# A retention layer in front of two MLPs: the first chunks' scores weighted by a decay table instead of scaled q and v

## The chip, the cores and the metric

The kernel runs on one core of one Trainium2 chip. The time is the device time of one execution in microseconds (us); the span of a profile is the part of it from the first to the last instruction. The engines are TensorE (PE; its weight loads PEld), VectorE (DVE), ScalarE (ACT), GpSimd (POOL) and SyncE (SP), which issues nearly all transfers.

## The reference

Four sequences of 768 positions with 8 heads of 64 channels go through a retention layer: per head a 64x64 state decays by a constant gamma at each position and takes in the outer product of k and v; the output is q times the state, scaled. The result, 3072 tokens of 512 channels, goes through a first MLP (512 to 2048, squared ReLU, back to 512) and a second (RMS norm, gate and value of 1536 with SiLU, back to 512). All is float32.

```python
state = gamma[None, :, None, None] * state + np.einsum('bhd,bhe->bhde', k[:, :, t], v[:, :, t])
y[:, :, t] = scale * np.einsum('bhd,bhde->bhe', q[:, :, t], state)
...
h = np.maximum(x @ w_in, 0.0)
return (h * h @ w_out).astype(np.float32)
...
xn = x / rms * rms_g
return (silu * val @ w_out).astype(np.float32)
```

## The kernel before

**Tiling.** Positions are cut into chunks of 128. Chunk c holds part c // 4 of sequence c % 4, so chunks 0 to 3 are the first parts of the four sequences and have no state in front of them. Four chunks make a block of 512 tokens; there are six blocks. Float32 products of the MLPs are made from two halves of each operand: a high half (a cast by ScalarE to float32r) and a low half (the rest, subtracted by VectorE: `low`, L74). `mm3` (L155) makes three products of each pair; the first needs both high halves, the second the low half of the moving operand, the third the low half of the weights. So 12 products of 512 columns make one `proj` (L165) or one `out1` (L189).

**Retention of a chunk.** `decay_q` multiplies q by the table `qdec_sb` (gamma to the i+1, with the scale), `decay_v` multiplies v by `vdec_sb` (gamma to the -1-j; eight small activations where ScalarE does it). `scores` makes k times q for eight heads into two PSUM banks, and VectorE multiplies them by the triangle `tri_sb` into P (L532). `values` multiplies v with P (L554) and, from chunk 4 on, adds the state's part (L560). `take_x` splits the result into the halves of the MLP's input x. `into_state` multiplies k with the scaled v (L544), and `take_state` scales that into the sequence's state by four activations (L577); `show_state` copies the state to where `values` reads it.

**Weights.** They come as 64-bit words of which the kernel takes float32 values apart: `fetch` loads a tile (512 KB) into one of three buffers, `magnitude` is one ScalarE activation, `convert` three VectorE instructions (L125 to L129), after which it issues the fetch of the tile three further on; `finish1` makes the halves of a first-MLP tile (ScalarE cast L94, VectorE low). The order of the tiles is i0, i1, o0, i2, o1, i3, ... (i for the first matrix, o for the second). One `tick` finishes a tile, takes the magnitude of the tile two later and converts the one after it; `low_first` says whether the low half comes before that convert on VectorE.

**Order.** The schedule is written out by hand: each engine, and SP's queue of transfers, works through its instructions in the order in which the code issues them. A transfer waits until the transfer eight before it has landed. The opening loads qdec, the twelve q, k and v tiles of chunks 0 to 3 (256 KB each) and, among them, the first two weight tiles, then k once more in natural layout for the states, and the tiles of chunks 4 and 5; the fourth weight tile comes after all of these. The opening scales q and v of chunks 0 to 3, makes their scores and values, keeps TensorE busy with products that nobody reads (`keep_warm`, L590), and makes all four chunks' state products in the four banks "acc" just before the first MLP starts.

`block1(j, ...)` (L664) is the first MLP over one block: for f = 0 to 15 it does `early` (a tick), the product with tile i(f), `act1` on ScalarE (ReLU, square, cast), `late` (a tick), the low half `s` on VectorE, and then `tail1`, the product of the f before with tile o(f-1) into the four "acc" banks. In the first block the scores of chunks 4, 5, 6, 7 stand at f = 2, 6, 10, 13, their values one f later, and the next chunk's `decay_v` and `decay_q` two f later. `first_states(f)` (L639) is called last before `tail1` in block 0: at f = 0 it scales all four states and q of chunk 4, at f = 1 it scales v of chunk 4 and shows its state.

Of the kernel before, what the change touches and what calls it, by code (L numbers as in the profile page):

```python
# [21 lines left out]
C = 128  # L22
# [23 lines left out]
def retention_then_two_mlps(  # L46
    ctx: ExitStack, tc: tile.TileContext, qT, kT, kn, vn, w1i, w1o, w2g, w2v, w2o, rmsg, tri, qdec, vdec, sdec, out
# [393 lines left out]
    with tc.manual_schedule():  # L441
        nc.vector.memset(ones, 1.0)

        with ExitStack() as rctx:
# [14 lines left out]
            def put(c, qq, k_, vv, kk, *more):  # L459
                nc.sync.dma_start(qq, qT[c])  # L460
                nc.sync.dma_start(k_, kT[c])
                if more:
                    nc.sync.dma_start(*more)
                nc.sync.dma_start(vv, vn[c])
                chunk[c] = (qq, k_, vv, kk)
# [22 lines left out]
            def stage(c, *more):  # L488
# [4 lines left out]
                put(c, qq, k_, vv, kk, *more)  # L493
# [26 lines left out]
            def scores(c, tags, early=False):  # L520
# [10 lines left out]
                for h in range(2):  # L531
                    nc.vector.tensor_tensor(  # L532
                        out=P[:, h], in0=sc[h], in1=tri_sb.unsqueeze(1).to_broadcast([128, NP, C]), op=ALU.mult
# [13 lines left out]
            def values(c, tag, bufs):  # L547
# [4 lines left out]
                for p in range(NP):  # L552
                    for h, b in enumerate(heads):
# [27 lines left out]
            nc.sync.dma_start(qdec_sb, qdec)  # L581
            stage(0, vdec_sb, vdec)
# [10 lines left out]
            nc.sync.dma_start(tri_sb, tri)  # L593
            stage(1)
            fetch(0)
            stage(2)
            stage(3)
            fetch(1)
            nc.sync.dma_start(sdec_sb, sdec)
            for c in range(CB):  # L600
                nc.sync.dma_start(chunk[c][3], kn[c])
            fetch(2)
            nc.sync.dma_start(g_sb, rmsg)
            load(CB)
            load_q(CB)
            load_k(CB)
            load(CB + 1)
# [3 lines left out]
            decay_q(0, nc.vector)  # L611
            decay_v(0, nc.scalar)
            decay_q(1, nc.vector)
            scores(0, early_banks, early=True)
            keep_warm(WARM // 2)
            decay_v(1, nc.scalar)
            scores(1, early_banks, early=True)
            xs.append(values(0, "xs", 1))
            decay_q(2, nc.vector)
            magnitude(0)  # L620
            decay_v(2, nc.scalar)
            scores(2, early_banks, early=True)
            decay_q(3, nc.vector)
            take_x(0, cur, xs[0])
            xs.append(values(1, "sc", 1))
            convert(0)
            at[0] = 1
            scores(3, early_banks, early=True)
            decay_v(3, nc.scalar)
            take_x(1, cur, xs[1])  # L630
# [258 lines left out]
```

## Time and profile before

| | us |
|---|---|
| median of three runs (lowest, highest) | 1191.67 (1189.5, 1191.94) |
| the profiled execution, its own time | 1191.49 |
| its span | 1189.7 |
| PE busy in the span | 1166.1 |
| DVE busy | 711.6 |
| ACT busy | 571.0 |

Busy time is time in which an engine has at least one instruction in work; an engine idles where it waits. The views read here are the page, the timeline (one row for an instruction or a run of equal ones, with the idle time in front of it and what ended that in brackets), the chain of waits (followed back from a late instruction to what released it) and the busy time by stretch. Starts are in us from the span's start.

### The profile page before, as it was taken

The page shows a single profiled execution, that of the slowest core. Times are in us where ns is not written, and L with a number is a line of the kernel's source. Part 1 is how long each engine was busy: PE and PEld are TensorE (multiplying, and loading weights), DVE is VectorE, ACT ScalarE, POOL GpSimd, SP SyncE. Part 2 cuts the span into 40 slices and gives each one's busy share as a digit, 9 for nine tenths or more (in the row PEclk, how much of TensorE's full clock was granted, in tenths as well). Part 3 has the DMA queues.
Part 4 walks back from the last instruction along what each step waited for, and adds up shares of the span by engine and source line. Part 5 has one row for each costly group of instructions (what it writes and reads, how often), then busy time and mean ns, then how long its engine had stood idle before and what let it go on. Part 6 is the DMA issues. An engine that isn't in the chain of part 4 may idle for free.

```text
span 1189.7 us, 15526 instructions
## 1 busy us (share of the span) xinstructions
PE 1166.1 (98%) x6006; PEld 951.7 (80%) x6006; DVE 711.6 (60%) x1097; ACT 571.0 (48%) x1085; POOL 96.7 (8%) x76
## 2 busy tenths in 40 slices
PE   7999999999999999999999999999999999999998
PEld 6678888888888887887778877878788888888887
DVE  6999643363454335422655878774777775777740
ACT  5888544444443443434555444534544534544431
POOL 0000410040140004002000111000000000000000
PEclk9999999999999999999999999999999999999999
DMA  9666633352353234203032111132111132111001
GB/s 312 201 207 204 194 117 89 96 171 89 112 168 111 89 108 159 85 22 120 22 106 93 58 45 60 48 112 83 36 36 45 36 124 93 41 36 45 27 1 71
DMA packets 56618, 115.13 MB, mean 97 GB/s; under 512 B 6344, under 2 KB 12640, under 8 KB 56544
## 3 DMA queue, kind: packets, MB, share of 16 engines
q1 hardware_dynamic: 56544, 114.14, 30.2%
q8 instruction: 47, 0.77, 0.3%
q14 instruction: 27, 0.22, 0.1%
HBM read 92.09 MB, written 22.03 MB: 96 GB/s over the span
## 4 chain that ended last, share of the span: by engine, by line
PE 83%; DVE 9%; ACT 4%; DMA 2%; issue 1%; SPq 0%; DVEq 0%; ACTq 0%
PE acc L156 7%; PE acc L157 6%; PE acc L158 6%; PE h L156 6%; PE h L158 6%; PE h L157 6%; PE a L156 5%; PE a L158 5%; PE a L157 5%; PE b L156 3%; PE b L157 3%; PE b L158 3%; PE late L156 3%; PE late L158 3%; PE late L157 3%; PE oacc L157 2%
## 5 line engine op out<-in xcount | busy, mean ns | idle before, releaser
L74 DVE TENSOR_TENSOR s<-r,s 128x512 fp32r<-128x512 f32 x96 | 70.0, 729 | 205.6 <-ACT s L186 205.6
L183 ACT ACTIVATE r<-h 128x512 f32<-128x512 f32 x96 | 57.2, 596 | 209.7 <-PE h L158 209.7
L156 PE MATMUL acc<-s,w_o 128*128 128x512 f32 x384 | 154.1, 401 | 2.5 <-ACT st L577 1.7
L157 PE MATMUL acc<-s,w_o 128*128 128x512 f32 x384 | 150.5, 392 | 4.5 <-DVE s L74 4.4
L158 PE MATMUL h<-xh,w_i 128*128 128x512 f32 x384 | 149.6, 390 | 0.9 <-DVE w_i L74 0.9
L156 PE MATMUL h<-xh,w_i 128*128 128x512 f32 x384 | 150.3, 391 | 0.0
L158 PE MATMUL acc<-s,w_o 128*128 128x512 f32 x384 | 149.9, 390 | 0.0
L157 PE MATMUL h<-xl,w_i 128*128 128x512 f32 x384 | 149.5, 389 | 0.0
L156 PE MATMUL a<-xop,ring 128*128 128x512 f32 x288 | 112.7, 391 | 4.3 <-DVE t L369 4.3
L158 PE MATMUL a<-xop,ring 128*128 128x512 f32 x288 | 112.1, 389 | 0.0
L157 PE MATMUL a<-xop,ring 128*128 128x512 f32 x288 | 112.1, 389 | 0.0
L157 PEld LDWEIGHTS acc<-s,w_o 128*128 128x128 f32 x384 | 72.2, 188 | 20.5 <-DVE s L74 6.9
L156 PEld LDWEIGHTS acc<-s,w_o 128*128 128x128 f32 x384 | 72.1, 188 | 20.2 <-ACT st L577 3.0
L158 PEld LDWEIGHTS h<-xh,w_i 128*128 128x128 f32 x384 | 72.1, 188 | 16.6 <-DVE w_i L74 1.6
L156 PEld LDWEIGHTS h<-xh,w_i 128*128 128x128 f32 x384 | 72.1, 188 | 16.2 <-issue 1.0
L156 PE MATMUL b<-xop,ring 128*128 128x512 f32 x216 | 84.3, 390 | 0.2
L158 PEld LDWEIGHTS acc<-s,w_o 128*128 128x128 f32 x384 | 72.1, 188 | 15.1
L158 PE MATMUL b<-xop,ring 128*128 128x512 f32 x216 | 84.1, 389 | 0.0
L157 PE MATMUL b<-xop,ring 128*128 128x512 f32 x216 | 84.1, 389 | 0.0
L157 PEld LDWEIGHTS h<-xl,w_i 128*128 128x128 f32 x384 | 72.1, 188 | 14.8
L74 DVE TENSOR_TENSOR ring<-q,ring 128x512 fp32r<-128x512 f32 x90 | 57.4, 687 | 36.6 <-ACT ring L77 36.6
L156 PEld LDWEIGHTS a<-xop,ring 128*128 128x128 f32 x288 | 54.1, 188 | 17.7 <-DVE t L369 6.6
(154 smaller groups left out, 2170.3 us busy)
## 6 DMA issues: line engine op xcount, KB each, us to landing
q<-wq SPq DMA_DIRECT2D x72, 256.0 KB, 3.3
raw<-w1i SPq DMA_DIRECT2D x16, 512.0 KB, 4.0
raw<-w1o SPq DMA_DIRECT2D x16, 512.0 KB, 3.7
raw<-w2g SPq DMA_DIRECT2D x12, 512.0 KB, 3.5
raw<-w2v SPq DMA_DIRECT2D x12, 512.0 KB, 3.4
raw<-w2o SPq DMA_DIRECT2D x12, 512.0 KB, 3.6
wq<-f SPq DMA_DIRECT2D x24, 256.0 KB, 4.5
out<-o SPq DMA_DIRECT2D x24, 256.0 KB, 2.1
```

The lines of the kernel that those rows point to most:

```text
L74: eng.tensor_tensor(out=dst_l, in0=src, in1=dst_h.bitcast(F32), op=ALU.subtract)
L156: nc.tensor.matmul(acc, ah, bh, start=start, stop=False, **more)
L157: nc.tensor.matmul(acc, ah, bl, start=False, stop=False, **more)
L158: nc.tensor.matmul(acc, al, bh, start=False, stop=stop, **more)
L183: nc.scalar.activation(r, h, AF.Relu)
```

## The change

- P of chunks 0 to 3 is made from unscaled q: VectorE multiplies the scores by a table `decays` instead of by the triangle. For two positions j and i of a head the table holds 0 where j > i, and else the product of what `vdec` has for j and `qdec` for i. It is made on the chip: two TensorE products of eight rows (`vrow`, one row per head, and `qrow`, which holds each head's row in its own block of columns), 128 by 512 each, and two VectorE multiplies by the triangle. `vrow`, `qrow` and the triangle are loaded on ScalarE's queue.
- `values` of chunks 0 to 3 uses unscaled v, and takes the heads in another order. v is scaled afterwards, for the states alone: chunk 0 and 1 between the `take_x` of the opening, chunk 2 at its end, chunk 3 at f = 3.
- The first weight tile is the first load of SP's queue; `vdec` and `sdec` come after the second weight tile, `qdec` after the third. The natural k of chunks 1 to 3 is loaded after the tiles of chunk 4.
- The first weight tile is converted before the first scores; its low half stands between the scores of chunks 1 and 2. In the first ticks the low half goes ahead of the convert.
- The state products of chunks 0 to 3 are made one at a time in the bank "xs", at f = 0, 2, 5 and 9, each followed by its `take_state`. `first_states` is called before the next chunk's `decay_v` and `decay_q`; `decay_q` of chunk 4 moves from f = 0 to f = 1.

```diff
--- before.py
+++ after.py
@@ -44,7 +44,7 @@
 
 @with_exitstack
 def retention_then_two_mlps(
-    ctx: ExitStack, tc: tile.TileContext, qT, kT, kn, vn, w1i, w1o, w2g, w2v, w2o, rmsg, tri, qdec, vdec, sdec, out
+    ctx: ExitStack, tc: tile.TileContext, qT, kT, kn, vn, w1i, w1o, w2g, w2v, w2o, rmsg, tri, qdec, vdec, sdec, vrow, qrow, out
 ):
     nc = tc.nc
 
@@ -456,11 +456,9 @@
             chunk, pt = {}, {}
             heads = [slice(0, D), slice(D, 2 * D)]
 
-            def put(c, qq, k_, vv, kk, *more):
+            def put(c, qq, k_, vv, kk):
                 nc.sync.dma_start(qq, qT[c])
                 nc.sync.dma_start(k_, kT[c])
-                if more:
-                    nc.sync.dma_start(*more)
                 nc.sync.dma_start(vv, vn[c])
                 chunk[c] = (qq, k_, vv, kk)
 
@@ -485,12 +483,12 @@
                     chunk[c][1] = rp.tile([128, NP, C], F32, tag="kT", name="kTt", bufs=1)
                     nc.sync.dma_start(chunk[c][1], kT[c])
 
-            def stage(c, *more):
+            def stage(c):
 
                 t = [wp.tile([128, 2, 512], F32, tag="w", name=f"stage{c}{i}") for i in range(2)]
                 qq, k_ = (t[0][:, i, :].rearrange("p (a i) -> p a i", a=NP) for i in range(2))
                 vv, kk = (t[1][:, i, :].rearrange("p (a h d) -> p a h d", a=NP, h=2) for i in range(2))
-                put(c, qq, k_, vv, kk, *more)
+                put(c, qq, k_, vv, kk)
 
             def decay_q(c, eng):
                 if c < NCH:
@@ -530,7 +528,10 @@
                         nc.tensor.matmul(sc[h][:, p, :], k_[b, p, :], qq[b, p, :], start=True, stop=True)
                 for h in range(2):
                     nc.vector.tensor_tensor(
-                        out=P[:, h], in0=sc[h], in1=tri_sb.unsqueeze(1).to_broadcast([128, NP, C]), op=ALU.mult
+                        out=P[:, h],
+                        in0=sc[h],
+                        in1=decays[:, h] if early else tri_sb.unsqueeze(1).to_broadcast([128, NP, C]),
+                        op=ALU.mult,
                     )
                 pt[c] = P
 
@@ -549,8 +550,8 @@
                 qq, _, vv, _ = chunk[c]
                 xs = bank(tag, [128, NP, C], "xs", bufs)
 
-                for p in range(NP):
-                    for h, b in enumerate(heads):
+                for h, b in enumerate(heads):
+                    for p in range(NP):
                         nc.tensor.matmul(
                             xs[b, p, :], vv[:, p, h, :], P[:, h, p, :], start=(p == 0),
                             stop=(c < B and p == NP - 1), skip_group_check=True,
@@ -578,8 +579,17 @@
                         st[n][:, p, :], (st[n] if c >= B else kv)[:, p, :], AF.Copy, scale=sdec_sb[:, p:p + 1]
                     )
 
-            nc.sync.dma_start(qdec_sb, qdec)
-            stage(0, vdec_sb, vdec)
+            decays, rows_q, rows_v = (wp.tile([128, 2, 512], F32, tag="w", name=n) for n in ("decays", "qr", "vr"))
+            decays = decays.rearrange("p h (a i) -> p h a i", a=NP)
+            fetch(0)
+            nc.scalar.dma_start(rows_v[:H, 0, :C], vrow)
+            nc.scalar.dma_start(rows_q[:H].rearrange("p h n -> p (h n)"), qrow)
+            nc.scalar.dma_start(tri_sb, tri)
+            for c in range(CB):
+                stage(c)
+            fetch(1)
+            nc.sync.dma_start(vdec_sb, vdec)
+            nc.sync.dma_start(sdec_sb, sdec)
             nc.vector.memset(st_in, 0.0)
             nc.scalar.copy(st[0][:, 0, :PQ], ones)
 
@@ -590,61 +600,64 @@
                     nc.tensor.matmul(warm, ones, st_in[:, 0, :], start=True, stop=True)
 
             keep_warm(WARM)
-            nc.sync.dma_start(tri_sb, tri)
-            stage(1)
-            fetch(0)
-            stage(2)
-            stage(3)
-            fetch(1)
-            nc.sync.dma_start(sdec_sb, sdec)
-            for c in range(CB):
-                nc.sync.dma_start(chunk[c][3], kn[c])
+
+            db = [bank("acc", [128, NP, C], "db", 4) for _ in range(2)]
+            for h in range(2):
+                nc.tensor.matmul(
+                    db[h].rearrange("p a i -> p (a i)"), rows_v[:H, 0, :C], rows_q[:H, h, :], start=True, stop=True
+                )
+                nc.vector.tensor_tensor(
+                    out=decays[:, h], in0=db[h], in1=tri_sb.unsqueeze(1).to_broadcast([128, NP, C]), op=ALU.mult
+                )
+            keep_warm(WARM // 2)
+            nc.sync.dma_start(chunk[0][3], kn[0])
             fetch(2)
-            nc.sync.dma_start(g_sb, rmsg)
+            nc.sync.dma_start(qdec_sb, qdec)
             load(CB)
             load_q(CB)
             load_k(CB)
+            for c in range(1, CB):
+                nc.sync.dma_start(chunk[c][3], kn[c])
+            nc.sync.dma_start(g_sb, rmsg)
             load(CB + 1)
             cur = new_x()
 
             xs = []
-            decay_q(0, nc.vector)
+            magnitude(0)
+            convert(0)
+            scores(0, early_banks, early=True)
+            low0 = finish1(w1_keys[0], done.pop(0))
+            scores(1, early_banks, early=True)
+            low0()
+            xs.append(values(0, "xs", 1))
+            scores(2, early_banks, early=True)
+            take_x(0, cur, xs[0])
             decay_v(0, nc.scalar)
-            decay_q(1, nc.vector)
-            scores(0, early_banks, early=True)
-            keep_warm(WARM // 2)
+            xs.append(values(1, "sc", 1))
+            scores(3, early_banks, early=True)
+            take_x(1, cur, xs[1])
             decay_v(1, nc.scalar)
-            scores(1, early_banks, early=True)
-            xs.append(values(0, "xs", 1))
-            decay_q(2, nc.vector)
-            magnitude(0)
-            decay_v(2, nc.scalar)
-            scores(2, early_banks, early=True)
-            decay_q(3, nc.vector)
-            take_x(0, cur, xs[0])
-            xs.append(values(1, "sc", 1))
-            convert(0)
-            at[0] = 1
-            scores(3, early_banks, early=True)
-            decay_v(3, nc.scalar)
-            take_x(1, cur, xs[1])
             xs.append(values(2, "h", 2))
+            take_x(2, cur, xs[2])
             xs.append(values(3, "h", 2))
-            take_x(2, cur, xs[2])
             magnitude(1)
             take_x(3, cur, xs[3])
-            kvs = [into_state(c, "acc", 4) for c in range(CB)]
-            tick(low_first=True)
+            convert(1)
+            magnitude(2)
+            at[0] = 2
+            decay_v(2, nc.scalar)
 
             def first_states(f):
 
-                if f == 0:
-                    for c in range(CB):
-                        take_state(c, kvs[c])
-                    decay_q(CB, nc.vector)
+                for c, n in enumerate((0, 2, 5, 9)):
+                    if f == n:
+                        take_state(c, into_state(c, "xs", 1))
                 if f == 1:
                     decay_v(CB, nc.scalar)
+                    decay_q(CB, nc.vector)
                     show_state(CB)
+                if f == 3:
+                    decay_v(CB - 1, nc.scalar)
 
             prev = None
             at_chunk = CB
@@ -691,14 +704,14 @@
                         take_state(at_chunk, kv)
                         load_q(at_chunk + 1)
                         load(at_chunk + 2)
+                    if j == 0:
+                        first_states(f)
                     if f in v_at:
                         decay_v(at_chunk + 1, nc.gpsimd if j else nc.scalar)
                         show_state(at_chunk + 1)
                     if f in q_at:
                         decay_q(at_chunk + 1, nc.gpsimd if j else nc.vector)
                         at_chunk += 1
-                    if j == 0:
-                        first_states(f)
                     while f and ("o", f - 1) not in W:
                         tick()
                     tail1("h", 2)
@@ -708,7 +721,7 @@
 
             def early1(f):
                 if at[0] <= n1_steps or f % 2 == 0 or f // 2 < per_block - NF1 // 2:
-                    tick()
+                    tick(low_first=at[0] < 4)
                     if at[0] in (5, 10):
                         tick()
 
@@ -836,6 +849,11 @@
     vdec = GAMMA[None, :] ** (-1.0 - i[:, None])
     sdec = GAMMA[:, None] ** float(C)
 
+
+    qrow = np.zeros((H, H, C))
+    for r in range(H):
+        qrow[r, r] = qdec[r % NP * 2 + r // NP]
+
     def per_pair(a):
         return np.repeat(a.reshape(NP, 2, -1), D, axis=1).transpose(1, 0, 2)
 
@@ -844,6 +862,8 @@
         "qdec": np.ascontiguousarray(per_pair(qdec), np.float32),
         "vdec": np.ascontiguousarray(vdec, np.float32),
         "sdec": np.ascontiguousarray(per_pair(sdec)[:, :, 0], np.float32),
+        "vrow": np.ascontiguousarray(vdec.T.reshape(NP, 2, C).swapaxes(0, 1).reshape(H, C), np.float32),
+        "qrow": qrow.reshape(H, H * C).astype(np.float32),
     }
 
 
```

## Rows read from the trace of the kernel before

**Rows 1.** Page, part 1: busy time, share of the span, instructions per engine.
```profile
PE 1166.1 (98%) x6006; PEld 951.7 (80%) x6006; DVE 711.6 (60%) x1097; ACT 571.0 (48%) x1085; POOL 96.7 (8%) x76
```

**Rows 2.** Stretches: length, busy us (instructions) by engine, granted clock, DMA share, GB/s.
```profile
22.40:61.40 39.00, 33.72 (x179) 25.08 (x178) 36.01 (x63) 30.79 (x75) 0.00 (x0) 1.00 0.67 214
...
61.40:125.00 63.60, 63.42 (x396) 51.85 (x397) 58.98 (x101) 51.02 (x110) 0.00 (x0) 1.00 0.64 206
```

**Rows 3.** Chain of waits, 60 to 63 us: start, length, engine, tile, line.
```profile
61.84 0.23 PE acc L158
```

**Rows 4.** Timeline of PE: start, busy, engine, line, op, out<-in, count, [idle before].
```profile
22.39 0.50 PE L156 MATMUL h<-xh,w_i 128*128 128x512 f32 x1
...
31.09 0.50 PE L156 MATMUL acc<-s,w_o 128*128 128x512 f32 x1 [1.75 <-ACT st L577]
...
37.30 1.16 PE L530 MATMUL sc<-qnt,kTt 64*128 64x128 f32 x16
...
40.17 0.50 PE L157 MATMUL acc<-s,w_o 128*128 128x512 f32 x1 [1.28 <-DVE s L74]
...
54.58 0.50 PE L157 MATMUL acc<-s,w_o 128*128 128x512 f32 x1 [0.34 <-DVE s L74]
...
61.34 0.50 PE L157 MATMUL acc<-s,w_o 128*128 128x512 f32 x1 [1.01 <-DVE s L74]
```

**Rows 5.** Timeline of DVE, 20 to 75 us.
```profile
21.25 0.69 DVE L74 TENSOR_TENSOR xl<-xs,xh 128x512 fp32r<-128x512 f32 x1 [0.67 <-ACT xh L77]
...
22.46 0.42 DVE L125 TENSOR_SCALAR f<-f 128x512 int32<-128x512 int32 x1
...
24.25 0.42 DVE L125 TENSOR_SCALAR f<-f 128x512 int32<-128x512 int32 x1
...
30.29 0.68 DVE L74 TENSOR_TENSOR s<-r,s 128x512 fp32r<-128x512 f32 x1
...
30.89 0.69 DVE L497 TENSOR_TENSOR qnt<-qnt,qdec_sb 128x512 f32<-128x512 f32 x1
...
34.03 0.69 DVE L74 TENSOR_TENSOR w_i<-f,w_i 128x512 fp32r<-128x512 f32 x1 [0.67 <-ACT w_i L94]
```

**Rows 6.** Timeline of ACT, 0 to 75 us.
```profile
13.19 2.02 ACT L506 ACTIVATE stage<-stage,vdec_sb 128x64 f32<-128x64 f32 x8 [0.73 <-DMA stage<-vn]
...
26.66 0.66 ACT L120 ACTIVATE f<-raw 128x512 f32<-128x512 f32 x1 [1.68 <-DMA raw<-w1i]
...
27.23 0.58 ACT L183 ACTIVATE r<-h 128x512 f32<-128x512 f32 x1
...
30.12 3.37 ACT L577 ACTIVATE st<-kv,sdec_sb 128x64 f32<-128x64 f32 x16
...
55.49 1.07 ACT L577 ACTIVATE st<-st,sdec_sb 128x64 f32<-128x64 f32 x4 [2.11 <-DVE st L575]
...
56.46 0.61 ACT L94 CAST w_i<-f 128x512 fp32r<-128x512 f32 x1
```

**Rows 7.** Timeline of SP's queue, 0 to 75 us (issue of a transfer).
```profile
9.87 0.33 SPq L115 DMA_DIRECT2D raw<-w1i  x1
...
16.51 0.33 SPq L476 DMA_DIRECT2D vnt<-vn  x1
```

**Rows 8.** Stretches of the opening, columns as in rows 2.
```profile
0.00:15.10 15.10, 11.73 (x110) 9.59 (x110) 6.43 (x12) 8.02 (x27) 0.20 (x4) 1.00 0.87 299
...
0.00:25.00 25.00, 19.78 (x233) 16.62 (x234) 15.48 (x27) 14.45 (x43) 0.20 (x4) 1.00 0.92 328
...
10.00:24.00 14.00, 10.53 (x171) 9.03 (x168) 11.44 (x20) 10.18 (x32) 0.00 (x0) 1.00 1.05 391
```

**Rows 9.** Timeline of PE, the opening.
```profile
1.49 4.47 PE L590 MATMUL warm<-st_in,ones 128*32 128x128 f32 x20 [1.49 <-DVE st_in L583]
...
7.57 1.28 PE L590 MATMUL warm<-st_in,ones 128*32 128x128 f32 x10
...
20.36 2.10 PE L544 MATMUL kv<-stage 128*64 128x64 f32 x62
```

## Prediction

> **What bounds the kernel now.** I read the busy shares first: TensorE is busy 1166.1 of 1189.7 us [rows 1], so all of its idle time together is some 24 us, and only that and TensorE's own work can be won. Then busy time by stretch [rows 2]: from 22.4 to 61.4 us VectorE is busy 36.0 of 39.0 us and TensorE 33.7; from 61.4 to 125 us TensorE is busy 63.4 of 63.6. There the chain of waits steps from product to product by 0.23 us [rows 3]. So the change, which ends in the first block (to about 125 us), can be worth only what it moves TensorE's position at 61.4 us, less what it adds to TensorE's work behind that point. The timeline of TensorE shows where it stood before: first product of the first MLP at 22.39, first output product at 31.09, the next output products at 40.17, and at 61.34 [rows 4]. The last two rows name VectorE's `s`, the "low" half of the activation, as what came last. VectorE in turn is fed by ScalarE, and ScalarE stood still 1.68 us for the load of the fourth weight tile (tile 3), which came at 26.66 [rows 6].
>
> I call the weight tiles 0, 1, 2, ... in the order of loading (i0, i1, o0, i2, o1, ...). What follows is a walk through the in-order streams of VectorE, ScalarE and TensorE: an instruction starts when its engine is free and its inputs have ended, with the distance from start to start of the rows. For VectorE that is 0.60 for one 128x512 tensor operation (30.29 to 30.89), a mask too, and 1.79 for a convert of three instructions (22.46 to 24.25) [rows 5]; for ScalarE 0.57 for a magnitude (26.66 to 27.23), 2.89 for the five 512-column instructions from act1(0) to the state activations (27.23 to 30.12), 0.24 for each of the eight activations of a `decay_v` (2.02 in all), 0.21 for each of the four of a `take_state` [rows 6]; for TensorE 2.74 for twelve products of 512 columns [rows 3]. The same walk through the kernel before gives 40.18 and 61.30 for the two `s` waits, against 40.17 and 61.34 in the rows.
>
> **The opening, up to the first product.** Off VectorE go four `decay_q` (4 x 0.60 = 2.4 us); on it come two table multiplies (1.2). The two table products have eight rows and 512 float32 columns, a form that the trace lacks. By the warm-up products, which have 128 columns in two instructions each (4.47 us for 20 early, 1.28 for 10 later [rows 9]), one table costs four such products: 1.0 to 1.8 us. They stand behind the ten warm-up products, which end at 5.96, so the tables are ready between 8.6 and 10.2; I take 8.6, by the later, nearer row. VectorE then has convert(0) 1.8, eight masks 4.8, low(0) and x low(0) 1.2, and would have the last mask out at 17.0 (two short waits for scores included), or 18.8 with the slow tables, which is hidden by what follows.
>
> What follows is ScalarE's order: x high(0), `decay_v(0)`, x high(1), `decay_v(1)`, x high(2), magnitude(1), x high(3). `decay_v` needs `vdec_sb`, whose load went out fourth before and now stands behind 4.30 MB (tile 0 and tile 1 with 0.52 each, twelve chunk loads of 0.26, tri and tables 0.1). Before, 299 GB/s over 15.1 us are 4.51 MB [rows 8], so 4.30 MB are through at 14.5; and the load of tile 1, whose last byte by the same count (4.53 MB) went at 15.1, released a load that waited for it on SP's queue, the first `vnt`, at 16.51 [rows 7], 1.4 later. So vdec lands at 15.9. Then `decay_v(0)` 15.9 to 17.8, x high(1), `decay_v(1)` 18.3 to 20.2, x high(2), magnitude, x high(3) 21.3 to 21.9, and its low half ends at 22.6. Before, it began at 21.25 and ended at 21.94, but the state products (2.1 us) kept TensorE until 22.39 [rows 4, 5, 9]. The first product thus starts at 22.6 instead of 22.39: the saved VectorE work is lost to vdec. Bounds: 14.8 to 16.5 for the landing (all early bytes at the later 391 GB/s [rows 8]; 0.6 late), x ready 21.5 to 23.2.
>
> [...]
>
> **The fourth weight tile.** As before it is the last of the first loads on SP's queue: in front of it now are 8.20 MB plus 0.04 of tables, before 8.20 with it. 328 GB/s over 25 us are 8.20 MB [rows 8]; ScalarE sees it at 26.66. That three small loads go through ScalarE's queue does not take bytes off. I take 26.6; bounds 24.7 (early bytes at 391 GB/s) to 27.3. ScalarE waits here again in front of act1(0). VectorE meanwhile: convert(1) 22.5 to 24.4, low(1) behind the cast 25.0 to 25.6 (it now precedes convert(2)), convert(2), convert(3) to 29.2, low(2) 29.6, `s` low(0) 30.2 to 30.9; before it ended at 30.9 as well. Output products(0) then flow without the four waits for `take_state` (sixteen activations, 3.37 us, at 30.12 before [rows 6]): they end 0.4 earlier.
>
> **f = 1 and 2.** `decay_q(4)` has left f = 0 (0.6 us of VectorE) and ScalarE does four state activations there, not sixteen, so low(3) no longer waits 0.67 for its cast, as at 34.03 [rows 5]: `s` low(1) ends at 38.7, before 40.1. That is the gain, 1.5 us. But `decay_q(4)` now stands right behind it, 38.6 to 39.3, and scores(4), before at 37.30 [rows 4], waits for it: TensorE is done with product(2) at 36.1 and idles 3.2 us. Scores 1.09, the state product of chunk 1 0.5 (by 2.10 us for 62 instructions, 16 each [rows 9]), and output products(1) start at 40.9; before they flowed as from 39.94 (40.17 with one product done ahead). TensorE is 0.9 late, VectorE 0.9 early. Up to f = 3 TensorE no longer meets the wait at 54.58 [rows 4], which cost it 0.5 with the product that ran ahead, nor the small ones before it, and comes out 0.1 ahead.
>
> **f = 3 to 5.** `decay_v(3)`, 2.0 us on ScalarE, now stands behind `take_state(4)`. In the rows ScalarE goes from that state's activations at 55.49 straight into the cast at 56.46, and act1(4) is one cast and one magnitude later [rows 6]. Now `take_state(4)` runs from 54.6 (0.9 early), `decay_v(3)` 55.6 to 57.5, cast 57.5, act1(4) 58.6; VectorE waits 1.8 for the cast; `s` low(4) ends at 62.3, before 61.3. The state product of chunk 2 lies in TensorE's wait. So TensorE goes on at 62.3 instead of 61.34: **+1.0 us**. The price of `decay_v(3)` in this is 1.9 (without it VectorE would be 0.9 ahead). Behind that the streams keep their distances; the state product of chunk 3 at f = 9 adds 0.5 and falls into a wait of TensorE for `decay_q(7)` near 113. `take_state(2)` and `(3)` lie in ScalarE's waits. Nothing after the block is touched.
>
> **Sum.** 1191.49 of the profiled run + 1.0 = 1192.5; the median of the runs shown, 1191.67, is 0.2 above that run. With the early bounds of both loads the walk gives -0.5, with vdec out of the way altogether -0.9, with the late ones +1.7. About 0.2% (2.4 us) is what a measurement can tell from no change, so the forecast is no change.
>
> **Rivals.** (1) Slower: the clock. TensorE idles from 18.0 to 22.6 (last values product to first MLP product), while the longest wait that stands in its rows was 1.75 [rows 4]. The rows have the granted clock at 1.00, the level of 2.4 GHz, in all these stretches [rows 2, 8], yet the warm-up products right after the start, when TensorE had done nothing, took 0.224 us each against 0.128 later [rows 9], near the two to one of 1.2 GHz. The mechanism is a first product at the low level at 22.6. Twelve products then take 5.5 us instead of 2.7, and some of the second twelve follow: 3.5 us in all. 1.8 of it hides, because act1(0) waits for tile 3 anyway; the rest, 1.7, delays `s` low(0) and all behind it: +2.7, 1194.2, and with the late load 1194.9. It decides from the point where product(0) ends after 27.2. For it: the 4.6 us; against it: no wait in the rows is that long, and behind those of 1.0 to 1.75 the products keep 0.23 apart. The Trainium skill (TensorE: Matmul & The Clock Gate, Part 1) says that the array falls to 1.2 GHz after an idle stretch, which would be this case.
> (2) Faster: the loads come at their early bounds and `decay_v(3)` costs nothing because ScalarE has less in front of it than I count: -0.9 - 1.9 = -2.8, 1188.7. For it: VectorE's work in the opening is 1.2 us less, and ScalarE's waits for VectorE sum to several us; against it: ScalarE's wait at 55.49 is in front of `decay_v(3)`, not behind.
> (3) The move of `decay_q(4)` does not hold scores(4) because VectorE is further ahead: 0.9 less at f = 2, but the wait at f = 5 takes it back; the end stays at +1.0, 1192.5.
>
> **Chances.** Forecast with the bounds of the loads 0.48, (3) 0.08, (1) 0.22, (2) 0.22. The likeliest's own range is 1190.6 to 1193.4; to (1) and (2) it reaches from 1188.9 to 1194.9. Faster by over 0.2%: 0.22; within: 0.56; slower: 0.22.
>
> **What would show it.** After: vdec's first `decay_v` on ScalarE at 15.9 after a wait for a DMA; x ready at 22.6 with TensorE idle over 4 us in front; the magnitude of tile 3 at 26.6; scores(4) at 39.3 waiting for `decay_q`; `decay_v(3)` between 55 and 58 and `s` low(4) ending near 62.3. I am wrong if tile 3 is there before 24.5, if `s` low(4) ends before 60, if the first product runs 0.4 us apart instead of 0.23, or if TensorE waits behind 65 us.

## The result, and the profile after

The changed kernel takes 1200.97 us (median of 4 runs, 1200.3 to 1202.13) against 1191.49 (4 runs, 1189.5 to 1191.94) for the kernel before: ratio 1.0084, 95% interval 1.0066 to 1.0101. It is 0.84% slower, where no change was forecast, with 1194.9 at the end of the range. (The ratios here and below come with their intervals and need not equal the quotient of the two medians, which is 1.0080 here.)

The profiled span is 1198.5 us, before 1189.7. The page's busy times, after (before: [rows 1]):
```profile
PE 1178.9 (98%) x6010; PEld 964.1 (80%) x6010; DVE 710.0 (59%) x1095; ACT 570.9 (48%) x1085; POOL 94.1 (8%) x76
```
The span is 8.8 us longer, and TensorE is 12.8 us longer busy, with four more instructions on record. VectorE and ScalarE do what they did. So this is no new wait: TensorE itself needs longer for the same products.

Where it needs longer, the stretches of [rows 2] and two later ones show (length, busy us and instructions of PE, PEld, DVE, ACT, POOL, granted clock, DMA share, GB/s), after:
```profile
22.40:61.40 39.00, 35.95 (x223) 28.11 (x222) 34.82 (x60) 31.96 (x77) 0.00 (x0) 0.96 0.66 208
61.40:125.00 63.60, 63.10 (x400) 51.65 (x401) 58.58 (x100) 51.84 (x115) 0.00 (x0) 1.00 0.62 198
125.00:550.00 425.00, 425.00 (x2426) 347.68 (x2426) 179.18 (x260) 182.09 (x349) 75.96 (x58) 1.00 0.36 111
```
and the third of them before:
```profile
125.00:550.00 425.00, 425.00 (x2461) 346.33 (x2460) 181.04 (x261) 185.08 (x352) 80.79 (x61) 1.00 0.36 111
```
From 125 to 550 us TensorE is busy all the time in both, at a granted clock of 1.00, and gets through 35 instructions fewer after the change. This is behind the first block, where the prediction said that nothing is touched.

To place the loss in time I take one instruction that each of the 96 steps of the first MLPs has once, ScalarE's cast of `s` (L186), and subtract its start before from its start after, number by number: -0.55 us at number 0, +0.55 at 4, +0.56 at 8, +2.12 at 14, +3.10 at 18, +10.40 at 78, +10.36 at 94. Up to number 8 (84 us) the walk holds. From number 15 (+2.61) to 78 the 16 chunks 8 to 23 add 0.487 each. Numbers 4, 78 and 94, before:
```profile
58.82 0.62 ACT L186 CAST s<-r 128x512 fp32r<-128x512 f32 x1
...
535.32 0.62 ACT L186 CAST s<-r 128x512 fp32r<-128x512 f32 x1
...
626.74 0.62 ACT L186 CAST s<-r 128x512 fp32r<-128x512 f32 x1
```
and after:
```profile
59.37 0.62 ACT L186 CAST s<-r 128x512 fp32r<-128x512 f32 x1
...
545.72 0.62 ACT L186 CAST s<-r 128x512 fp32r<-128x512 f32 x1
...
637.10 0.62 ACT L186 CAST s<-r 128x512 fp32r<-128x512 f32 x1
```
What takes 0.49 us longer is `values`. TensorE's timeline of one chunk, before and then after:
```profile
166.78 1.05 PE L554 MATMUL xs<-Pt,vnt 128*64 128x128 f32 x16
167.75 1.16 PE L560 MATMUL xs<-qnt,st_in 128*128 128x128 f32 x8
```
```profile
169.88 1.53 PE L555 MATMUL xs<-Pt,vnt 128*64 128x128 f32 x16
171.34 1.16 PE L561 MATMUL xs<-qnt,st_in 128*128 128x128 f32 x8
```
The same eight products (two instructions each) take 0.97 us from their start to that of the next product before, and 1.46 after. One instruction alone did not get longer; all of that line, after (count: minimum, median and maximum in ns; the 64 of the opening are listed apart):
```profile
L555 PE MATMUL xs<-Pt,vnt x320: 272/273/323, 46.8 to 537.5; 128*64 128x128 f32 x160
```
The line before has 272/273/323 as well. So it is the overlap of neighbours that went. The sixteen start 0.061 us apart before (0.97 / 16) and 0.091 after. The change turned two loops around: before, pairs of heads outside and the two heads of a pair inside, so that the products write by turns into the lower and the upper 64 rows of `xs`; after, one head's four pairs first, so that four products in a row write the same 64 rows. The index that the inner loop holds still, the head, also picks the half of P that is read and the columns of v; no run here separates these from the half of `xs`. The weight loads of the sixteen (PEld) spread with them, from 0.86 to 1.34 us, so the traces do not say whether a load or a product waits. 320 instructions are 20 chunks behind the opening, and 20 x 0.49 = 9.8 us.

Not all of it lengthens the run, and two other terms stand in the sum. TensorE's scores of chunks 5, 6 and 7, before:
```profile
66.80 1.16 PE L530 MATMUL sc<-qnt,kTt 64*128 64x128 f32 x16
...
92.47 1.16 PE L530 MATMUL sc<-qnt,kTt 64*128 64x128 f32 x16
...
112.97 1.16 PE L530 MATMUL sc<-qnt,kTt 64*128 64x128 f32 x16 [0.18 <-PE h L158]
```
and after, with the state product of chunk 3 between the first two:
```profile
67.34 1.16 PE L528 MATMUL sc<-qnt,kTt 64*128 64x128 f32 x16
...
88.08 0.69 PE L545 MATMUL kv<-stage 128*64 128x64 f32 x16
...
94.36 1.16 PE L528 MATMUL sc<-qnt,kTt 64*128 64x128 f32 x16
...
115.10 1.16 PE L528 MATMUL sc<-qnt,kTt 64*128 64x128 f32 x16
```
They start 0.54, 1.89 and 2.13 us later. In front of the first, the `values` of chunk 4 at 46.8 us were taken up by TensorE's wait for `s` (0.56 us at 61.90, 1.01 before). Between the first and the second stand the `values` of chunk 5 and the state product of chunk 3, which therefore costs 0.86 us; the run e1 below, with the old order, has the same 0.86 there (0.62 to 1.48). Between the second and the third the `values` of chunk 6 add 0.49, and 0.25 are won back where the kernel before waits and the changed one does not. So 0.54 + 0.86 - 0.25 and 19 x 0.487 = 9.25 make the +10.40 at number 78.

The span is only 8.8 longer because the kernel before loses 1.55 us late, which the changed kernel does not: from the `tot` products below to the end of the span it takes 402.7 us before, 401.1 after. Behind a wait of 2.21 us the products before ran 0.43 us apart for a while, with a granted clock of 0.94 from 770 to 800 us (after: 1.00),
```profile
787.01 0.43 PE L235 MATMUL tot<-sq,ones 128*32 128x128 f32 x8 [2.21 <-DVE t L369]
...
789.07 0.63 PE L156 MATMUL late<-wp,xl 128*128 128x512 f32 x1
789.50 0.63 PE L157 MATMUL late<-wp,xl 128*128 128x512 f32 x1
789.93 0.63 PE L158 MATMUL late<-wp,xl 128*128 128x512 f32 x1
```
and after, behind the same wait, they did not:
```profile
797.36 0.43 PE L235 MATMUL tot<-sq,ones 128*32 128x128 f32 x8 [2.20 <-DVE t L369]
797.71 0.50 PE L156 MATMUL late<-wp,xh 128*128 128x512 f32 x1
798.05 0.40 PE L157 MATMUL late<-wp,xh 128*128 128x512 f32 x1
```

### The profile page after: what moved, and what is told of

Read it like the earlier page. It is cut to its first block, busy times and chain, and to the rows that moved or that the text cites. A ratio compares the mean times of both kernels' runs of the same rounds, so it can differ in the third digit from the quotient of the medians.

```text
span 1198.5 us, 15528 instructions
## 1 busy us (share of the span) xinstructions
PE 1178.9 (98%) x6010; PEld 964.1 (80%) x6010; DVE 710.0 (59%) x1095; ACT 570.9 (48%) x1085; POOL 94.1 (8%) x76
## 4 chain that ended last, share of the span: by engine, by line
PE 83%; DVE 9%; ACT 4%; DMA 3%; issue 1%; SPq 0%; ACTq 0%; DVEq 0%
PE acc L156 7%; PE acc L157 6%; PE acc L158 6%; PE h L156 6%; PE h L157 6%; PE h L158 6%; PE a L156 5%; PE a L158 5%; PE a L157 4%; PE b L156 3%; PE b L158 3%; PE b L157 3%; PE late L156 3%; PE late L158 3%; PE late L157 3%; PE oacc L158 2%
```

## The experiments

Theory A: the time is the turned loops. Rivals: B, at first that the clock and the moved state products make the loss, and from e3 on that the price is one per neighbour in the same half (so short runs cost in proportion); C, the low clock after idle stretches decides what is left; D, against C, what is left has another cause, or the clock's loss is hidden by later waits. All ratios are to the kernel before, timed on the same chip.

**e1_heads_inner**: the changed kernel with the old order of the loops.
```diff
-                for h, b in enumerate(heads):
-                    for p in range(NP):
+                for p in range(NP):
+                    for h, b in enumerate(heads):
```


> The changed kernel with only the order of the values products put back (four pairs outside, the two heads of a pair inside). Theory A (the order): with both heads of a pair alternating between the two 64-row halves of the output, sixteen products take 0.97 us from start to start; with one head's four pairs first they take 1.46, 0.49 more, in each of the 20 chunks behind the opening where TensorE never waits: 9.8 us come back, the kernel is at 0.999 to 1.002 of the kernel before (+0.5 us by the walk with the measured landings). Theory B (the clock and the moved state products make the loss, the order only shows it): at most 3 us come back, 1.005 or more.

Measured: 1191.08 us (11 runs), ratio 1.0003 (0.9995 to 1.0012). All of the loss is gone:
```profile
168.01 1.04 PE L555 MATMUL xs<-Pt,vnt 128*64 128x128 f32 x16
168.99 1.16 PE L561 MATMUL xs<-qnt,st_in 128*128 128x128 f32 x8
```
Its last `s` cast is 0.74 us behind that of before, where the changed kernel's is 10.36 behind: 9.62 us from the order alone, 9.8 by the count. At number 80 it is 9.17, near the 9.25 of the sum above; what adds 0.45 behind that, I did not take apart.

**e2_before_heads_outer**: the reverse, the kernel before with the new order and nothing else.
```diff
-                for p in range(NP):
-                    for h, b in enumerate(heads):
+                for h, b in enumerate(heads):
+                    for p in range(NP):
```


> The kernel before with only the order of the values products changed to that of the changed kernel. Theory A: 20 x 0.49 = 9.8 us slower, and up to 0.5 more where the opening shows it: ratio 1.008 to 1.009. Theory B: no change, 1.000 to 1.002.

Measured: 1200.03 us (4 runs), ratio 1.0070 (1.0055 to 1.0086):
```profile
169.10 1.53 PE L554 MATMUL xs<-Pt,vnt 128*64 128x128 f32 x16
170.56 1.16 PE L560 MATMUL xs<-qnt,st_in 128*128 128x128 f32 x8
```
The last `s` cast is 9.69 us behind that of before. The ratio lies below the expected 1.008 to 1.009, which its interval reaches. The loop order makes the loss without any other part of the change, and taking it back removes it. That is shown from both sides.

**e3_before_pairs**: the kernel before with runs of two in one half.
```diff
-                for p in range(NP):
-                    for h, b in enumerate(heads):
+                for p, h, b in [(p2 + p, h, b) for p2 in (0, 2) for h, b in enumerate(heads) for p in range(2)]:
```


> The kernel before with the values products in pairs: two of one head, two of the other, twice over. If the price is per neighbour that writes the same half of the output (6 of 7 steps with one head first, none when they alternate, 4 of 7 in pairs), 4/6 of 0.49 = 0.33 us a chunk, 6.5 us, ratio 1.0055. If what counts is that the four pairs of a head run in one group whose end the other head waits for, it is between 0 and 0.1 us a chunk: ratio below 1.002.

Measured: 1192.62 us (10 runs), ratio 1.0009 (1.0000 to 1.0019):
```profile
167.02 1.10 PE L553 MATMUL xs<-Pt,vnt 128*64 128x128 f32 x16
168.04 1.16 PE L559 MATMUL xs<-qnt,st_in 128*128 128x128 f32 x8
```
1.02 us, 0.05 more than by turns, as the second of the two expectations had it. B, with a price per neighbour, is refuted: four neighbours in one half cost 0.05 here, six cost 0.49 above.

**e8_before_threes**: runs of three, then single ones.
```diff
-                for p in range(NP):
-                    for h, b in enumerate(heads):
+                for p, h, b in [(p, h, b) for r in ((0, 1, 2), (3,)) for h, b in enumerate(heads) for p in r]:
```


> The kernel before with the values products in runs of three of one head, three of the other, then one and one. Runs of two cost 0.06 us of 0.49 a chunk. If what counts is how far ahead TensorE finds a product of the other half, three (six instructions) lie between two (four) and four (eight): 0.1 to 0.4 us a chunk, sixteen products 1.10 to 1.45 us. If the whole loss comes only when one half has no products left to pair with, it is as with runs of two, 1.10.

Measured: 1198.15 us in one run, span 1196.4, the last `s` cast 6.65 us behind that of before, 1.09 of it from the opening:
```profile
168.77 1.31 PE L553 MATMUL xs<-Pt,vnt 128*64 128x128 f32 x16
170.02 1.16 PE L559 MATMUL xs<-qnt,st_in 128*128 128x128 f32 x8
```
1.25 us, 0.28 more than by turns, again with four neighbours, and 20 x 0.28 is 5.6 us. So it goes with the length of the run: 0.97, 1.02, 1.25, 1.46 us for runs of one, two, three, four. Both halves have a third product here and a third and a fourth above; beyond the 0.05 of the runs of two that is 0.23 / 2 and 0.44 / 4, about 0.11 us for each third or fourth product. Why a second one is nearly free is not shown.

**e4_heads_outer_opening**: the changed kernel with the new order only in the four chunks of the opening.
```diff
-                for h, b in enumerate(heads):
-                    for p in range(NP):
+                order = [(p, h, b) for h, b in enumerate(heads) for p in range(NP)]
+                if c >= B:
+                    order = [(p, h, b) for p in range(NP) for h, b in enumerate(heads)]
+                for p, h, b in order:
```


> The changed kernel with the heads outside only for chunks 0 to 3, where the products of one head may start before the mask of the other is done, and inside for all others. Theory A: within 0.5 us of the kernel with the order put back everywhere (0.999 to 1.002 of the kernel before), since the opening is held by the landing of vdec and of the fourth weight tile, not by the values products. Theory B: as the first of these runs under B, 1.005 or more.

Measured: 1192.54 us (11 runs), ratio 1.0009 (1.0000 to 1.0017). The later chunks are back at 0.97 us. In the opening the sixteen last 1.58 us, and the last `values` ended 0.73 us ahead of the first MLP product, so there they are on the path; but they stand behind tables that came late in this execution,
```profile
5.90 3.77 PE L608 MATMUL db<-qr,vr 8*128 8x512 f32 x4
9.60 2.34 PE L602 MATMUL warm<-st_in,ones 128*32 128x128 f32 x10
...
23.54 0.50 PE L156 MATMUL h<-xh,w_i 128*128 128x512 f32 x1 [0.73 <-ACT xh L77]
```
3.77 us against 1.95 in the changed kernel, and the first MLP product at 23.54 us against 21.16. It was TensorE as a whole: the ten warm-up instructions behind the tables took 2.34 us (1.28 in e1), the 32 of the first scores 3.23 (2.06 in e1). So this trace does not price the opening's order apart from the slow start. Its eleven times fall in two groups: five from 1190.53 to 1191.08, about e1's median, and six from 1192.54 to 1193.14, among them the profiled one.

**e5_v3_in_gap** (e1 with `decay_v(3)` moved into ScalarE's wait ahead of `take_state(4)`):
```diff
-                if f == 3:
-                    decay_v(CB - 1, nc.scalar)
...
                         take_x(at_chunk, ret, xs)
+                        if at_chunk == CB:
+                            decay_v(CB - 1, nc.scalar)
                         take_state(at_chunk, kv)
```


> The changed kernel with the order of the values products put back, and v of chunk 3 scaled not behind the state of chunk 4 but in front of it, where ScalarE waited 2.3 us for VectorE. Theory A (the walk of the prediction is right in the small terms: this scaling costs 1.9 us at f = 4): 1.9 us faster than the order put back alone, ratio 0.998 to 0.9995 to the kernel before. Theory C (the small terms are not what is left; the low clock of TensorE after its idle stretches is): no different from it, 1.000 to 1.001.

Measured: 1192.14 us (11 runs), ratio 1.0010 (1.0001 to 1.0019). No gain; the expectation of A fails. C's figure (1.000 to 1.001) is met, but that the clock is the reason is not shown by it. The `s` cast of step 4 does come earlier (1.54 us ahead of before, in e1 0.47 behind), but from step 14 on the run is where e1 is (+1.13 and +1.23). The stretch from 45 to 125 us, e5:
```profile
45.00:125.00 80.00, 80.00 (x524) 65.09 (x523) 73.04 (x126) 64.83 (x145) 0.00 (x0) 1.00 0.63 205
```
TensorE does not wait once in it, and in e1 neither. Once TensorE has stood still at scores(4) (2.87 us in both), it is the latest engine, and an earlier `s` frees nothing.

**e6_loads** (e1 with `vdec_sb` loaded fourth again, on ScalarE's queue, and with tile 3 ahead of the loads that only the states and chunk 5 want):
```diff
             nc.scalar.dma_start(tri_sb, tri)
+            nc.scalar.dma_start(vdec_sb, vdec)
...
-            nc.sync.dma_start(vdec_sb, vdec)
...
-            for c in range(1, CB):
-                nc.sync.dma_start(chunk[c][3], kn[c])
-            nc.sync.dma_start(g_sb, rmsg)
-            load(CB + 1)
...
             convert(0)
+            for c in range(1, CB):
+                nc.sync.dma_start(chunk[c][3], kn[c])
+            nc.sync.dma_start(g_sb, rmsg)
+            load(CB + 1)
```


> The changed kernel with the order of the values products put back and two loads moved: vdec as the fourth transfer on ScalarE's queue, and the fourth weight tile in front of the natural k of chunks 1 to 3 and the tiles of chunk 5. Theory A: x is ready near 19.6 instead of 21.9, tile 3 lands near 22 instead of 26.1, and TensorE is 2.6 us earlier at f = 5 than with the order put back alone: ratio 0.9975 to 0.999. Theory C: the idle stretches stay and with them the low clock, gain under 1 us, 0.9995 to 1.0005.

Measured: 1190.86 us (11 runs, 1188.97 to 1193.49), ratio 1.0003 (0.9994 to 1.0012). The walk is right about the loads: `decay_v(0)` at 13.61 with no wait, tile 3's magnitude at 22.91 instead of 26.09, first product at 19.57. Its profiled execution took 1189.04, near the lower end. The median shows none of it, as C expected, and the granted clock of each execution bears on it: the two with 0.999 took 1188.97 and 1189.04, the nine with 0.996 or 0.997 took 1189.61 to 1193.49. In the trace the wait for scores(4) was 3.03 us, and the clock 0.77 from 38 to 44 us.

**e7_all** (e1 with both of these, and `decay_q(4)` back at f = 0):
```diff
                 if f == 0:
                     decay_q(CB, nc.vector)
                 if f == 1:
                     decay_v(CB, nc.scalar)
-                    decay_q(CB, nc.vector)
                     show_state(CB)
```


> All of it: order put back, v of chunk 3 scaled in ScalarE's wait, q of chunk 4 scaled at f = 0 as before, vdec and the fourth weight tile loaded earlier. Theory A: 4.5 us faster than the order put back alone, about 3.5 to 4 us faster than the kernel before, ratio 0.9965 to 0.9975. Theory C: above 0.9985.

Measured: 1189.73 us (11 runs, 1187.21 to 1192.9), ratio 0.9992 (0.9981 to 1.0004): not told from no change. Yet in the trace the `s` casts stand 3.5 us ahead of before throughout (steps 14 to 80), and TensorE runs scores(4) at 33.28 without a wait. Its times are spread over 5.7 us, and its profiled one (1188.07) is a low one. That left open what the higher ones pay.

**e9_all_filled** (e7 with products that nobody reads, where TensorE stood idle) and **e10_heads_inner_filled** (e1 with more of them). Of e9:
```diff
             xs.append(values(3, "h", 2))
+            fill(3, "acc", 4)
...
+                    if j == 0 and f == 1:
+                        fill(3, "sc", 1)
                     tail1("h", 2)
```


> The run e7_all (order of the values as before, decay_v(3) into the gap, decay_q(4) at f=0, the loads earlier) with three products that nobody reads behind the last values of the opening (idle 0.8 us there) and three ahead of the first w_o product (idle 1.4 us), 1.34 us each time. Its times ran from 1187.2 to 1192.9 us, its profiled execution (1188.07, no low clock in it, first streams 3.5 us ahead of before) lies at the lower end. Theory C (the upper ones are executions in which the clock fell after one of these waits): the median comes to 1187.5 to 1188.8, ratio 0.9972 to 0.9985, and the spread shrinks to some 2 us. Rival D (the upper ones have another cause, such as transfers that land late in some executions): median 1189 to 1190.5, ratio 0.9985 to 1.0000, and the spread stays near 5 us.

> The changed kernel with the pairs outermost again (as in the run e1_heads_inner), and with products whose result nobody reads put where TensorE stood idle there: six behind the last values of the opening (idle 3.16 us before the first projection) and five ahead of the scores of chunk 4 (idle 2.87 us); by the warm products' 0.45 us each (4.47 us for ten) they fill 2.7 and 2.2 us of the waits. Theory C (the low clock after the idle stretch is what the opening pays: ten products 0.43 apart instead of 0.23 in e1's trace, 2.0 us, and again 0.7 us from the scores on): granted clock 1.00 through the first 60 us, the 0.43-apart stretch gone, 1.5 to 2.5 us less than e1's 1191.1, ratio to the kernel before 0.9980 to 0.9995. Rival D (the clock's loss is hidden by later waits on ScalarE and VectorE, or the low clock comes anyway): the time stays within 0.7 us of e1's, ratio 0.9997 to 1.0010.

Measured: e9 1186.76 us (6 runs, 1185.77 to 1189.22), ratio **0.9966 (0.9954 to 0.9978)**; e10 1191.26 us (11 runs), ratio 0.9999 (0.9990 to 1.0007). The intervals of e9 and e7 do not overlap. e9's granted clock was 1.00 up to 62 us. TensorE, e9:
```profile
18.58 0.84 PE L605 MATMUL fill<-tri_sb,ones 128*32 128x128 f32 x6
...
26.47 0.84 PE L605 MATMUL fill<-tri_sb,ones 128*32 128x128 f32 x6
...
28.14 0.50 PE L157 MATMUL acc<-s,w_o 128*128 128x512 f32 x1 [0.40 <-DVE s L74]
```
A product of two instructions took 0.28 us here, not 0.45, so the fillers in e10 left a wait, and the clock fell behind it all the same:
```profile
17.90 1.50 PE L605 MATMUL fill<-tri_sb,ones 128*32 128x128 f32 x12
20.73 0.50 PE L156 MATMUL h<-xh,w_i 128*128 128x512 f32 x1 [1.33 <-ACT xh L77]
```
```profile
22.00:24.00 2.00, 2.00 (x6) 1.53 (x5) 1.28 (x3) 1.78 (x6) 0.00 (x0) 0.50 0.96 370
```
So e10 is no test of a kept clock: C's forecast for it missed, because the clock was not kept, and its time is in the range of D, which allowed for that.

What made e9 faster than e7 is not settled. Its median and ratio lie below the range of C (0.9972 to 0.9985), and its spread is 3.5 us, not 2. For C: none of its six executions has a mean clock under 0.999, while four of e7's eleven have 0.997 or 0.998. Against C as the whole cause: e7's three highest times (1191.83, 1192.44 and 1192.9) have 0.999, as its four lowest (1187.21 to 1188.34) have; and e9's two highest (1189.2 and 1189.22) have 1.000, as its two lowest (1185.77 and 1185.96) have. So the mean clock does not separate the high times from the low; a slow start of TensorE as in e4, for which the view gives a clock of 1.00, is a candidate that no trace of these executions shows. Nor do the traces show the fillers at work: e7's clock was also 1.00 up to 62 us, e9's `s` cast at number 80 is 0.54 us later than e7's, and all of the 2.1 us between the two profiled spans is made behind that, where no filler stands: e9 is 0.5 us ahead at the `tot` products near 783 us, and gains another 1.6 behind them, where e7's clock fell and e9's did not. e9 and e7 were also timed on different chips.

## Why the prediction was wrong

The step that failed is the last sentence of "f = 3 to 5": "Behind that the streams keep their distances ... Nothing after the block is touched." The change turns the loops of `values`, and `values` runs for every chunk of the kernel. The list of the change names the new order with `values` of chunks 0 to 3; the diff turns it for all 24. It should have stood in the sum as a term of its own: 20 x the price of the order, with the price unknown. The prediction did state the test, "less what it adds to TensorE's work behind that point", and put nothing in. Measured, the term is 20 x 0.49 = 9.8 us: by the e1 and changed traces 9.62, and e2 shows it alone. With it the forecast would have been 1192.5 + 9.8 = 1202.3, against 1200.97. None of the signs of being wrong that the prediction lists came: all of them look at the opening and the first block.

A second term of the same paragraph was put at nothing: the state product of chunk 3, which was to add 0.5 and fall into a wait for `decay_q(7)` near 113 us. It cost 0.86, and that wait was 0.18 us long in the kernel before; 0.6 stayed. By the trace the profiled run is 1191.49 + 0.54 + 0.86 - 0.25 + 9.25 - 1.55 = 1200.3, as measured. The last term, the clock's fall in the kernel before, is no part of the change, so that 1202.3 lies as near to 1200.97 as it does is partly luck.

The other steps, by the trace after:

**Opening.** `decay_v(0)` after a wait for the DMA at 15.19 (forecast 15.9). The tables took 1.95 us for two, the lower end of 2.0 to 3.6. First product at 21.16 (22.6): the last wait in front of it is 1.08, not 4.6, because the slower `values` filled it; with the order taken back (e1) it is 3.16. ScalarE, after:
```profile
15.19 2.02 ACT L504 ACTIVATE stage<-stage,vdec_sb 128x64 f32<-128x64 f32 x8 [0.68 <-DMA vdec_sb<-vdec]
...
26.09 0.68 ACT L120 ACTIVATE f<-raw 128x512 f32<-128x512 f32 x1 [1.82 <-DMA raw<-w1i]
...
55.10 2.01 ACT L504 ACTIVATE stage<-stage,vdec_sb 128x64 f32<-128x64 f32 x8
57.02 0.60 ACT L94 CAST w_i<-f 128x512 fp32r<-128x512 f32 x1
```
**Tile 3** at 26.09 (26.6). With it and vdec earlier, the `s` casts of e6 are 2.0 us ahead of e1's from number 4 on, but its median is not; e6 moved both loads, so it does not price tile 3 alone. **scores(4)** waited for `decay_q(4)`, at 38.85 (39.3), and **`decay_v(3)`** stood at 55.10 to 57.0 (55.6 to 57.5) and held VectorE 1.77 us (1.8). TensorE, after, with the row that answers 61.34 of [rows 4]:
```profile
38.85 1.16 PE L528 MATMUL sc<-qnt,kTt 64*128 64x128 f32 x16 [1.27 <-DVE qnt L495]
...
61.90 0.50 PE L157 MATMUL acc<-s,w_o 128*128 128x512 f32 x1 [0.56 <-DVE s L74]
```
61.90 against a forecast of 62.3: the sum for the block is +0.56 instead of +1.0. The right size has a weaker ground than it seems. e5 shows that `decay_v(3)`, which I gave 1.9 us of the price, is worth nothing with the old loop order, because TensorE is late from the wait at scores(4) on: the walk named the right instruction at 61 us and the wrong cure.

**Rival (1)**, the clock, did happen, at other places than I put it. After, the granted clock was 0.66 from 7 to 12 us, and it was at the low level (near 0.5) around 32 us, behind waits of 0.90 and 0.83 us:
```profile
31.50:35.10 3.60, 3.60 (x10) 2.81 (x9) 3.51 (x6) 2.85 (x6) 0.00 (x0) 0.53 0.53 192
```
In e1 the first products behind the 3.16 us wait ran 0.43 apart, as the rival said: eight of them took from 21.96 to 25.48 us, 1.7 more than at 0.23, where the rival had 3.5 without a row for how long it lasts. e1 still came out at before's time. Against the rival stood that no wait in the rows was long; the trace of before had one, 2.21 us at 787 us, with products 0.43 apart behind it. **Rival (2)**, its loads early and `decay_v(3)` free, needed e6's and e5's edits, and its 2.8 us did not show in the times of either. **Rival (3)** did not occur: scores(4) did wait.

## What to carry to other kernels

Of a diff, list every function that it touches and count its calls in the whole kernel, not in the stage that the change is about; then ask of each reordered loop what the order does to neighbours on TensorE. Products like these, which fill only half of the output rows, should take the two halves by turns, or in runs of two at most; other shapes were not measured. Once TensorE is busy without a gap, an engine that waits less upstream is worth nothing, as in e5; look for the last place where TensorE itself stood still.

## What was not expected of the hardware

- Instructions of an unchanged 273 ns cost 0.061 or 0.091 us each by the order alone, with a step between runs of two (+0.05 us a chunk) and of three (+0.28).
- The clock's fall is not the same from one execution to the next. The wait of 2.20 to 2.21 us ahead of the `tot` products, near 783 to 797 us, stands in all twelve traces. Behind it products ran 0.43 us apart in six (before, e2, e3, e7, e8, e10) and in the other six not one did. The fall cost 1.4 to 1.6 us, by the time from there to the end of the span. Each trace is of another kernel, but the times of one kernel show it too: of 27 executions of the kernel before, timed with e5 to e8, 12 had a mean clock of 1.000 (median 1190.0 us), 10 had 0.999 (1191.0) and 5 had 0.997 (1191.8).
- A wait of 1.33 us was followed by the low level (e10, 22 us), one of 1.37 by none (e7, 27.78). The length of the last wait alone does not say it.
- TensorE's slow start ends at different times. The 20 warm-up instructions at 1.49 us took 3.69 to 4.48 us in these traces, 0.18 to 0.22 each, against 0.128 each for the ten later ones in most. In e4 the slow pace went on past 12 us: 3.77 us for two table products of eight rows, which took 1.95 in the changed kernel. The view gives a granted clock of 1.00 for all of this, so at the start the durations have to be read, not that column.
